# Keys and queries of the last two batches transposed by VectorE in 32x32 blocks instead of by TensorE

## The chip, the cores and the metric

The kernel runs on one core of a Trainium2 chip. The metric is the device time of one execution in microseconds; the median of three runs is given. The engines are named as in the profile: PE (TensorE, matrix products and their transpositions), PEld (its weight loads), DVE (VectorE), ACT (ScalarE), POOL (GpSimd) and SP (SyncE, which here only issues transfers). SBUF is the on-chip memory, PSUM the eight accumulator banks of PE.

## The reference

Attention with a sigmoid in place of a softmax feeds a gated product, and that feeds a soft mixture of experts. B = 4 batches, H = 12 heads, S = 448 tokens, D = 64.

```python
scores = q @ k.T / sqrt(64) - log(448)          # per batch and head, 448 x 448
x = sigmoid(scores) @ v                         # -> 1792 x 768 tokens
y = ((x @ w_a) * (x @ w_b)) @ w_out             # 768 -> 1536 -> 768
logits = y @ phi                                # 768 -> 32 slots
slot_in = softmax(logits, over tokens).T @ y    # 32 x 768, 4 slots for each of 8 experts
slot_out[e] = relu(slot_in[e] @ w1[e]) @ w2[e]
out = softmax(logits, over slots) @ slot_out
```

## The kernel before

Products are made in a split form: each operand is a high part (rounded) and a low part (the rest), and three products hi·hi, lo·hi, hi·lo are summed. So every K and Q is transposed, cast to `kh` or `qh`, and subtracted to `kl` or `ql`.

Attention is a generator, `att`, over 24 pairs g of heads (six a batch, pair g = 6b + p). For each pair:

- `load_qkv` loads K, Q and V three pairs ahead, from SP's queue, into rings of three buffers. K and Q lie in SBUF as 112 partitions by 4 chunks by 2 heads by 64, in runs of 256 bytes; K and V have four neighbouring tokens on one partition.
- `transposed` (L146) has PE turn the four 112x128 chunks into one PSUM bank of tag "ms" (L149), loads the next one, and sets the flag `run["trans"]`.
- `split_heads` makes the parts on DVE: `kh` at L142, `kl` at L143, and the same for Q. `emit_TK` does K, and for pairs above 12 Q as well; `emit_TQ` does Q of the earlier ones.
- `emit_S` (L183) makes the scores, chunk by chunk, two banks of tag "sc" for each (for chunk 2 of some pairs, tag "ab"), and ACT takes the sigmoid (L186).
- `emit_PV` (L196) makes 16 products with V into one "sc" bank, and `emit_x` copies the result (L219 on DVE, or ACT).

PSUM is shared by tags: four banks "sc", two "ms", two "ab", each handed out in turn, so that a new use of a bank waits for the last reader of the old one. In a pair from 13 on the order on PE is: K and Q of the next pair, chunk 0, PV of the last pair, chunks 1, 2, 3.

The pairs of batch 0 run first. Those of batch 1 are woven between the pieces of the gated product of batch 0, `ab(0)` (L520), until about 217 us. Batches 2 and 3 (pairs 12 to 23) follow nearly undisturbed until about 305 us; K and Q of pair 12 and 13 are still transposed inside `ab(0)`. Then come the products of batches 1 and 2 by a Strassen scheme (L692), `ab(3)`, and the experts, whose weights stream in from about 600 us on.

Until about 205 us DVE, ACT and POOL also bring the weights into another number format (L324, L328 on ACT, L335 to L337 on DVE, L342 on POOL), which is stored and loaded back and split (L436, L437).

The small work behind the gated product (group by group: adding to the logits at L475, transposing tokens at L489 with copies at L491, the first logits at L726, L750, L762, L771) is a list of generators, `fill`. After every step of attention or of `ab` one piece is taken from it by `fill_step`, unless that step has just transposed. The flag decides that:

```python
yield (fc * 12 + i * 6 + s * 2 + 2) / (KF * 12)
if not run.pop("trans", False):
    fill_step()
```

The dense loop over pairs 12 to 23 has the same two lines. Here a table of work does not set the order; the flag and the yields do.

Of the kernel before, what the change touches and what calls it, by code (L numbers as in the profile page):

```python
# [9 lines left out]
F32 = mybir.dt.float32  # L10
# [8 lines left out]
B, H, S, D = 4, 12, 448, 64  # L19
DM, FF, NS, NE, F = 768, 1536, 32, 8, 1024  # L20
C = 4
T = S // C
# [3 lines left out]
NP = H // 2  # L26
NE1, NE2 = 17, 4
ST0, PP, RAWS = 10, (3, 7), (2, 3, 10, 14)

LOW = 2.0 ** -15  # L30
HIGH = struct.unpack("f", struct.pack("I", 0x47EFFFFF))[0]
# [2 lines left out]
def body(ctx, tc, q, k, v, w_a, w_b, w_out, phi, w1, w2, out):  # L34
    nc = tc.nc
    pe, act, dve, pool, sp = nc.tensor, nc.scalar, nc.vector, nc.gpsimd, nc.sync
# [10 lines left out]
    atp = at_ctx.enter_context(tc.tile_pool(name="atp", bufs=1, side="right"))  # L47
# [14 lines left out]
    def ms(shape=(128, S)):  # L62
        tags = banks[run["banks"]]
        tag = tags[run["ms"] % len(tags)]
        run["ms"] += 1
        return ps_tile(tag, list(shape), 4 if tag == "sc" else 2)
# [49 lines left out]
    qkv_t = {}  # L116

    def load_qkv(g, names):
        if g >= B * NP:
            return  # L120
        b, p = divmod(g, NP)
        for src, nm, n in ((k, "k", 3), (q, "q", 3), (v, "v", 3)):
            if nm not in names:
                continue

            s = src[b, 2 * p:2 * p + 2].rearrange(
                "h (c p) d -> p h c d" if nm == "q" else "h (p c) d -> p h c d", c=C)
            if nm == "v":
                t = atp.tile([T, 2, C, D], F32, tag="vn", name="vn", bufs=n)
                sp.dma_start(out=t, in_=s)  # L130
            else:
                t = atp.tile([T, C, 2, D], F32, tag=nm + "n", name=nm + "n", bufs=n)
                for h in range(2):
                    sp.dma_start(out=t[:, :, h], in_=s[:, h])
            qkv_t[nm, g] = t
# [9 lines left out]

    def transposed(g, nm, t):  # L146
        a = qkv_t.pop((nm, g))
        for c in range(C):
            pe.transpose(t[:, c * T:(c + 1) * T], a[:, c].rearrange("p h d -> p (h d)"), ident[:T, :T])  # L149
        load_qkv(g + 3, nm)  # L150
        run["trans"] = True
        return t

    def emit_TK(g):
        if g >= B * NP:
            return
        both = g == 0 or g > 2 * NP
        tk = transposed(g, "k", ms())
        if both:
            tq = transposed(g, "q", ms())  # L160
        split_heads(g, "k", tk, dve.tensor_copy)
        if both:
            split_heads(g, "q", tq, dve.tensor_copy if g else act.copy)

    def emit_TQ(g):
        if g >= B * NP:
            return
        split_heads(g, "q", transposed(g, "q", ms()),
                    dve.tensor_copy)
# [43 lines left out]
    def emit_x(g):  # L213
        pv = pv_t.pop(g)
        qkv_t.pop(("v", g))
        b, kk = divmod(g, NP)
        if b:
            xt[g] = raw_x(b, kk)
            (act.copy if b == 1 else dve.tensor_copy)(xt[g], pv)  # L219
        else:  # L220
            xh = x0p.tile([128, S], F32R, tag=f"xh{kk}", name=f"xh{kk}")
            xl = x0p.tile([128, S], F32R, tag=f"xl{kk}", name=f"xl{kk}")
            act.activation(xh, pv, AF.Copy)
            dve.tensor_tensor(xl, pv, xh.bitcast(F32), op=ALU.subtract)
            xt[g] = (xh, xl)
        load_qkv(g + 3, "v")
# [693 lines left out]


    load_qkv(0, "qkv")
    consts()
    load_qkv(1, "qkv")
# [109 lines left out]
    for what in order0:  # L1034
        i = what[1]
        h, n, f0 = (0, 4, 4 * i) if i < 3 else (1, 6, 6 * (i - 3))
        for x in range(n):
            fc = f0 + x
            j = fc % 4
# [15 lines left out]
    for n in range(0, len(order1), 4):  # L1055
        _, g, x, _ = order1[n]
# [44 lines left out]
    for h in range(2):  # L1101
        for b in range(B):
            pl, nm = slots.pop(0)
# [4 lines left out]
    for h, (c0, w) in enumerate(COLS):  # L1108
# [4 lines left out]
        t = ms((128, w))  # L1113
        pe.matmul(t, selF.rearrange("p j s -> p (j s)"), s4[:, c0:c0 + w], start=True, stop=True)
        evac[h](s4r[:, c0:c0 + w], t)
        for c in range(C):
            op = []
            for b in range(B):
                tag = tags[k % 6]
# [35 lines left out]
```

## Time and profile before

| | |
|---|---|
| median of three runs | 702.97 us (702.44 to 703.36) |
| profiled execution | 703.76 us |
| its span in the trace | 702.0 us, mean granted clock 0.992 |
| PE busy | 657.9 us, 94% |
| PEld busy | 472.2 us, 67% |
| DVE busy | 368.4 us, 52% |
| POOL busy | 308.3 us, 44% |
| ACT busy | 297.6 us, 42% |
| chain that ended last | PE 66%, DMA 18%, DVE 6%, POOL 4%, ACT 2% |

The profile is of one execution, 0.8 us above the median; the time outside its span is 1.8 us. Busy shares are means over stages with different limits: a share of 52% may hide a stage in which an engine is always late.

### The profile page before, as it was taken

The page shows a single profiled execution, that of the slowest core. Times are in us where ns is not written, and L with a number is a line of the kernel's source. Part 1 is how long each engine was busy: PE and PEld are TensorE (multiplying, and loading weights), DVE is VectorE, ACT ScalarE, POOL GpSimd, SP SyncE. Part 2 cuts the span into 40 slices and gives each one's busy share as a digit, 9 for nine tenths or more (in the row PEclk, how much of TensorE's full clock was granted, in tenths as well). Part 3 has the DMA queues.
Part 4 walks back from the last instruction along what each step waited for, and adds up shares of the span by engine and source line. Part 5 has one row for each costly group of instructions (what it writes and reads, how often), then busy time and mean ns, then how long its engine had stood idle before and what let it go on. Part 6 is the DMA issues. An engine that isn't in the chain of part 4 may idle for free.

```text
span 702.0 us, 11034 instructions
## 1 busy us (share of the span) xinstructions
PE 657.9 (94%) x4187; PEld 472.2 (67%) x4187; DVE 368.4 (52%) x537; ACT 297.6 (42%) x536; POOL 308.3 (44%) x236
## 2 busy tenths in 40 slices
PE   6999999999999999999999999999998898997683
PEld 4557777777775555568988988998887786432132
DVE  4676899889754444449775675653322122300022
ACT  4888778779655465663333233202120011100021
POOL 0243767667644047339995575642333352000000
PEclk9999999999999999999999999999999999999997
DMA  9998999999834333201123323322999936999998
GB/s 197 254 294 215 278 312 302 279 278 304 245 120 129 71 98 77 71 0 46 46 85 103 99 73 98 116 68 80 256 391 413 379 114 240 374 416 415 409 350 276
DMA packets 104819, 146.90 MB, mean 209 GB/s; under 512 B 50880, under 2 KB 83904, under 8 KB 100800
## 3 DMA queue, kind: packets, MB, share of 16 engines
q1 hardware_dynamic: 101536, 139.81, 61.9%
q10 hardware_dynamic: 3232, 6.41, 2.7%
q8 instruction: 33, 0.54, 0.3%
q14 instruction: 18, 0.15, 0.1%
HBM read 122.69 MB, written 23.50 MB: 208 GB/s over the span
## 4 chain that ended last, share of the span: by engine, by line
PE 66%; DMA 18%; DVE 6%; POOL 4%; ACT 2%; issue 1%; SPq 0%; DVEq 0%; POOLq 0%; ACTq 0%
PE ab L520 15%; PE sc L692 14%; DMA e<-in_moe_w 9%; PE sc L196 9%; DMA wr<-ab 7%; PE ab L692 7%; PE sc L183 6%; PE ms L149 3%; PE ms L489 2%; DVE gk L337 2%; POOL wl L437 1%; PE ab L183 1%; DMA out<-w 1%; PE ms L471 1%; DVE gk L336 1%
## 5 line engine op out<-in xcount | busy, mean ns | idle before, releaser
L186 ACT ACTIVATE a<-sc,sums 112x448 f32<-112x448 f32 x158 | 89.0, 642 | 43.0 <-PE sc L183 42.7
L342 POOL TENSOR_TENSOR w<-gk,cy 128x768 int32<-128x768 int32 x36 | 66.2, 1840 | 91.5 <-DVE gk L337 59.6
L196 PE MATMUL sc<-a,vn 112*64 112x448 f32 x384 | 77.8, 546 | 1.0 <-ACT a L186 1.0
L437 POOL TENSOR_TENSOR wl<-wr,wh 128x768 fp32r<-128x768 f32 x22 | 40.5, 1842 | 68.3 <-DVE wh L436 43.2
L520 PE MATMUL ab<-t,wh 128*128 128x448 f32 x288 | 65.4, 372 | 5.3 <-DVE wh L436 5.3
L520 PEld LDWEIGHTS ab<-t,wh 128*128 128x128 f32 x288 | 52.8, 188 | 11.6 <-issue 5.3
L196 PEld LDWEIGHTS sc<-a,vn 112*64 112x64 f32 x384 | 25.7, 136 | 41.2 <-issue 34.8
L437 POOL TENSOR_TENSOR wl<-w,wh 128x768 fp32r<-128x768 f32 x24 | 44.3, 1848 | 2.5 <-ACT wh L436 2.5
L1086 PE MATMUL ab<-e,gk 128*32 128x384 f32 x240 | 33.3, 507 | 12.0 <-DMA e<-in_moe_w 12.0
L527 ACT COPY misc<-ab 128x448 f32<-128x448 f32 x24 | 12.8, 534 | 74.8 <-PE ab L520 38.6
L335 DVE TENSOR_SCALAR mf<-gk 128x768 f32<-128x768 f32 x36 | 34.1, 946 | 13.5 <-ACT gk L324 13.5
L183 PE MATMUL sc<-qh,kh 64*112 64x448 f32 x158 | 36.3, 429 | 1.1 <-ACT qh L142 0.6
L580 POOL TENSOR_TENSOR wx<-wr,wx 128x384 fp32r<-128x384 f32 x29 | 34.1, 1177 | 3.8 <-ACT wx L579 2.1
L436 DVE CAST wh<-wr 128x768 fp32r<-128x768 f32 x22 | 13.1, 594 | 42.3 <-DMA wr<-ab 41.1
L336 DVE TENSOR_SCALAR gk<-mf 128x768 uint32<-128x768 uint32 x36 | 34.3, 953 | 1.2
L520 PE MATMUL ab<-xh,wh 128*128 128x448 f32 x144 | 34.9, 378 | 0.0
L520 PE MATMUL ab<-xl,wh 128*128 128x448 f32 x144 | 34.5, 375 | 0.0
L520 PE MATMUL ab<-xh,wl 128*128 128x448 f32 x144 | 34.5, 375 | 0.0
L520 PE MATMUL ab<-t,wl 128*128 128x448 f32 x144 | 34.0, 372 | 0.0
L1086 PEld LDWEIGHTS ab<-e,gk 128*32 128x32 f32 x240 | 9.3, 112 | 35.0 <-DMA e<-in_moe_w 24.6
L580 POOL TENSOR_TENSOR wx<-T,wx 128x384 fp32r<-128x384 f32 x23 | 24.7, 1075 | 15.8 <-ACT wx L579 15.3
L520 PEld LDWEIGHTS ab<-xl,wh 128*128 128x128 f32 x144 | 26.0, 188 | 8.1 <-issue 6.3
(436 smaller groups left out, 1457.4 us busy)
## 6 DMA issues: line engine op xcount, KB each, us to landing
e<-in_moe_w SPq DMA_DIRECT2D x23, 1024.0 KB, 11.6
e<-in_moe_w SPq DMA_DIRECT2D x23, 768.0 KB, 15.1
wr<-ab SPq DMA_DIRECT2D x14, 768.0 KB, 4.8
ab<-w SPq DMA_DIRECT2D x24, 384.0 KB, 7.1
wr<-ab ACTq DMA_DIRECT2D x16, 384.0 KB, 7.5
kn<-in_k SPq DMA_DIRECT2D x48, 112.0 KB, 4.4
qn<-in_q SPq DMA_DIRECT2D x48, 112.0 KB, 4.1
vn<-in_v SPq DMA_DIRECT2D x24, 224.0 KB, 4.0
```

The lines of the kernel that those rows point to most:

```text
L149: pe.transpose(t[:, c * T:(c + 1) * T], a[:, c].rearrange("p h d -> p (h d)"), ident[:T, :T])
L183: pe.matmul(sc[h], kx[r, cs], qx[r], start=(i == 0), stop=(i == 2))
L186: act.activation(a, sc[h], AF.Sigmoid, bias=nlog[:T], scale=1.0 / math.sqrt(D))
L196: pe.matmul(pv_t[g][64 * h:64 * h + 64], qkv_t["v", g][:, h, c, :], a_t.pop((g, h, c)), start=(c == 0), stop=(c == C - 1))
L335: dve.tensor_scalar(mf, m, LOW, HIGH, op0=ALU.max, op1=ALU.min)
L336: dve.tensor_scalar(mi, mf.bitcast(U32), 3, 0x3FFFFFFF, op0=ALU.logical_shift_left, op1=ALU.bitwise_and)
L342: pool.tensor_tensor(thirds(w), m.bitcast(I32), thirds(cy_t.pop(x)), op=ALU.add)
L437: pool.tensor_tensor(wl, t, wh.bitcast(F32), op=ALU.subtract)
L520: pe.matmul(t, w[:, kk * 128:(kk + 1) * 128], xt[b * NP + kk][xi], start=(s == 0 and kk == 0), stop=(s == 2 and kk == KD - 1))
L580: pool.tensor_tensor(w[:, 1], t, w[:, 0].bitcast(F32), op=ALU.subtract)
L692: pe.matmul(t, w[:, wi, k * 128:(k + 1) * 128], xs[ORDER[m], k][xi], start=(s == 0 and k == 0), stop=(s == 2 and k == 2))
L1086: pe.matmul(sps[h][32 * j:32 * j + 32], hT[:, 2 * x + i, 2 * j + g], ring[order2[n + j]][0][:, i, c0:c0 + w], start=(g == 0 and x == 0 and ...
```

## The change

For pairs from GT0 = 12 on, K and Q are loaded by four transfers each: each fills 32 partitions with 14 runs of 32 numbers (128 bytes), so that one DVE instruction, `dve.transpose`, which turns every 32x32 block, gives the transposed 128x448 in the "ms" bank. V of these pairs is loaded in natural token order (runs of 256 bytes in place of 1 KB). `transposed` returns on that path without setting the flag.

```diff
+GT0 = 2 * NP
...
+            if g >= GT0:
+                if nm == "v":
+                    t = atp.tile([T, 2, C, D], F32, tag="vn", name="vn", bufs=n)
+                    sp.dma_start(out=t, in_=src[b, 2 * p:2 * p + 2].rearrange("h (c p) d -> p h c d", c=C))
+                else:
+                    t = atp.tile([128, 2 * C * D], F32, tag=nm + "n", name=nm + "n", bufs=n)
+                    t = t[:, :S].rearrange("p (n d) -> p n d", d=32)
+                    for j in range(4):
+                        sp.dma_start(out=t[32 * j:32 * j + 32],
+                                     in_=src[b, 2 * p + j // 2][:, j % 2 * 32:j % 2 * 32 + 32].rearrange(
+                                         "(n t) d -> t n d", t=32))
+                qkv_t[nm, g] = t
+                continue
...
-                t = atp.tile([T, C, 2, D], F32, tag=nm + "n", name=nm + "n", bufs=n)
+                t = atp.tile([128, 2 * C * D], F32, tag=nm + "n", name=nm + "n", bufs=n)
+                t = t[:T].rearrange("p (c h d) -> p c h d", c=C, h=2)
...
     def transposed(g, nm, t):
         a = qkv_t.pop((nm, g))
+        if g >= GT0:
+            dve.transpose(t, a.rearrange("p n d -> p (n d)"))
+            load_qkv(g + 3, nm)
+            return t
         for c in range(C):
             pe.transpose(t[:, c * T:(c + 1) * T], a[:, c].rearrange("p h d -> p (h d)"), ident[:T, :T])
         load_qkv(g + 3, nm)
```

Lines of the changed kernel stand some 15 to 19 further down: L142 is L157 there, L149 has no counterpart for these pairs (L164 on DVE), L183 is L202, L196 is L215, L337 is L356, L475 is L494, L489 is L508, L491 is L510, L520 is L539. A name's number is that of one allocation; allocations of one tag take its banks in turn, so `ms_2073` and `ms_2090` are one bank (two "ms" banks, `ms_2084` between them).

The first place is PE at K of pair 12, in `ab(0)`. The rows before, from the last L520 product ahead of K's transpositions to the group's transpositions behind PV:

```order
L520 MATMUL ab_2033<-xl5_752,wh2_1904 128x448
L149 MATMUL ms_2061<-ident_89,kn_1195 128x112 [waits DMAHW1_49,DMAHW0_49,DVE_49]
L149 MATMUL ms_2061<-ident_89,kn_1195 128x112 x3
L520 MATMUL ab_2033<-xh0_285,wl2_1905 128x448 [waits Pool_49]
...
L196 MATMUL sc_2087<-a_1919,vn_1228 64x448 [waits DMAHW4_49,Activation_49]
...
L489 MATMUL ms_2100<-ident_89,misc_95 112x128 [waits Activation_49]
L489 MATMUL ms_2100<-ident_89,misc_95 112x128 x3
L489 MATMUL ms_2106<-ident_89,misc_95 112x128 [waits DVE_49,PE_49]
L489 MATMUL ms_2106<-ident_89,misc_95 112x128 x3
```

And after:

```order
L539 MATMUL ab_2045<-xl5_752,wh2_1914 128x448
L508 MATMUL ms_2084<-ident_89,misc_95 112x128 [waits Activation_49]
L508 MATMUL ms_2084<-ident_89,misc_95 112x128 x3
L508 MATMUL ms_2090<-ident_89,misc_95 112x128 [waits DVE_49]
L508 MATMUL ms_2090<-ident_89,misc_95 112x128 x3
L539 MATMUL ab_2045<-xh0_285,wl2_1915 128x448 [waits Pool_49]
...
L215 MATMUL sc_2110<-a_1929,vn_1230 64x448 [waits DMAHW6_49]
```

The eight group transpositions move from behind PV to where K's four stood; their second four use the bank after K's and wait for DVE. The wait for POOL on the products behind them is the same.

The second place is DVE at the same point: the end of a weight's reformatting (L335 to L337), then the parts of K. Before:

```order
L335 TENSOR_SCALAR mf_2053<-gk_2_94 128x768 [waits Activation_49]
L336 TENSOR_SCALAR gk_2_94<-mf_2053 128x3x256 [waits DVE_49]
L337 SCALAR_TENSOR_TENSOR gk_2_94<-wr_all_96,gk_2_94 128x3x256 [waits DMAHW7_49,DVE_49]
L142 CAST kh_2069<-ms_2061 128x448 [waits PE_49]
L143 TENSOR_TENSOR kl_2070<-ms_2061,kh_2069 128x448 [waits DVE_49]
L530 TENSOR_TENSOR misc_95<-misc_95,ab_2033 128x448 [waits PE_49]
L491 COPY gk_01_93<-ms_2100 112x512 [waits PE_49]
```

And after:

```order
L354 TENSOR_SCALAR mf_2065<-gk_2_94 128x768 [waits Activation_49]
L355 TENSOR_SCALAR gk_2_94<-mf_2065 128x3x256 [waits DVE_49]
L356 SCALAR_TENSOR_TENSOR gk_2_94<-wr_all_96,gk_2_94 128x3x256 [waits DMAHW1_49,DVE_49]
L164 STREAM_TRANSPOSE ms_2073<-kn_1195 128x448 [waits DMAHW2_49]
L157 CAST kh_2080<-ms_2073 128x448 [waits DVE_49]
L158 TENSOR_TENSOR kl_2081<-ms_2073,kh_2080 128x448 [waits DVE_49]
L510 COPY gk_01_93<-ms_2084 112x512 [waits PE_49]
L549 TENSOR_TENSOR misc_95<-misc_95,ab_2045 128x448 [waits PE_49]
```

K's transposition is put between the reformatting and kh, and the copy of the group's tokens (L510) moves ahead of the product with the gate (L549).

The third place is PE in pair 14 (the transpositions are of pair 15), with the instructions of one shape drawn together. Before:

```order
L489 MATMUL ms<-ident,misc 112x128 x8
L149 MATMUL ms<-ident,kn 128x112 x4
L149 MATMUL ms<-ident,qn 128x112 x4
L183 MATMUL sc<-qh,kh 112x448 x2
L183 MATMUL sc<-qh,kl 112x448 x2
L183 MATMUL sc<-ql,kh 112x448 x2
L196 MATMUL sc<-a,vn 64x448 x8
L489 MATMUL ms<-ident,misc 112x128 x4
```

And after:

```order
L508 MATMUL ms<-ident,misc 112x128 x8
L202 MATMUL sc<-qh,kh 112x448 x2
L202 MATMUL sc<-qh,kl 112x448 x2
L202 MATMUL sc<-ql,kh 112x448 x2
L508 MATMUL ms<-ident,misc 112x128 x4
L215 MATMUL sc<-a,vn 64x448 x8
```

K's and Q's eight are gone, and the last four group transpositions move from behind PV to ahead of it.

## Rows read from the trace of the kernel before

**Rows 1.** Busy time by engine in one stretch: PE, PEld, DVE, ACT, POOL, clock, DMA, GB/s.

```profile
150.00:200.00 50.00, 48.97 (x302) 37.95 (x303) 43.53 (x51) 38.92 (x62) 33.31 (x19) 1.00 0.82 254
```

**Rows 2.** Timeline, 171 to 182 us: start, duration, engine, line, operation.

```profile
172.04 0.60 PE L149 MATMUL ms<-ident,kn 112*128 112x112 f32 x4 [0.22 <-DVE misc L475]
...
172.42 1.47 PE L520 MATMUL ab<-xh,wl 128*128 128x448 f32 x6
...
173.49 1.84 POOL L437 TENSOR_TENSOR wl<-w,wh 128x768 fp32r<-128x768 f32 x1
...
173.81 3.23 PE L196 MATMUL sc<-a,vn 112*64 112x448 f32 x16
173.87 2.28 DVE L337 SCALAR_TENSOR_TENSOR gk<-wr_all,gk 128x768 uint32<-128x768 uint32 x1
...
176.07 0.61 DVE L142 CAST kh<-ms 128x448 fp32r<-128x448 f32 x1
...
176.97 1.14 PE L489 MATMUL ms<-ident,misc 128*112 128x128 f32 x8
...
177.87 1.46 PE L520 MATMUL ab<-xh,wh 128*128 128x448 f32 x6
```

**Rows 3.** Timeline of PE, 192 to 202 us.

```profile
193.55 0.60 PE L149 MATMUL ms<-ident,qn 112*128 112x112 f32 x4 [0.24 <-ACT wT L368]
...
199.31 0.55 PE L149 MATMUL ms<-ident,kn 112*128 112x112 f32 x4
```

**Rows 4.** Timeline, 218 to 231 us.

```profile
218.24 0.39 DVE L603 CAST A12h<-t 128x448 fp32r<-128x448 f32 x1
...
224.56 0.52 ACT L750 COPY ls_d<-ab 128x448 f32<-128x448 f32 x1
...
225.54 0.46 PE L183 MATMUL ab<-qh,kh 64*112 64x448 f32 x2
...
226.95 1.08 PE L489 MATMUL ms<-ident,misc 128*112 128x128 f32 x8
...
227.63 1.29 DVE L491 COPY gk<-ms 112x512 f32<-112x512 f32 x2 [1.29 <-PE ms L489]
...
228.38 0.60 PE L149 MATMUL ms<-ident,kn 112*128 112x112 f32 x4 [0.35 <-DVE gk L491]
```

**Rows 5.** Timeline, 245 to 256 us.

```profile
253.77 0.60 PE L149 MATMUL ms<-ident,kn 112*128 112x112 f32 x4
...
254.69 0.46 PE L183 MATMUL sc<-qh,kh 64*112 64x448 f32 x2
...
254.81 1.70 ACT L186 ACTIVATE a<-sc,sums 112x448 f32<-112x448 f32 x3
...
255.51 0.20 PEld L196 LDWEIGHTS sc<-a,vn 112*64 112x64 f32 x4 [0.34 <-ACT a L186]
```

**Rows 6.** Costliest groups of the page: the sigmoids on ACT.

```profile
L186 ACT ACTIVATE a<-sc,sums 112x448 f32<-112x448 f32 x158 | 89.0, 642 | 43.0 <-PE sc L183 42.7
```

**Rows 7.** Timeline, 275 to 289 us.

```profile
281.38 0.46 PE L183 MATMUL sc<-qh,kh 64*112 64x448 f32 x1 [0.32 <-DVE t L219]
```

**Rows 8.** DMA queue in 247.3:254.2: packets, MB, share of 16 engines.

```profile
q1 hardware_dynamic: 2097, 0.69, 40.7%
```

**Rows 9.** The same view in 236:238.5.

```profile
q1 hardware_dynamic: 464, 0.06, 15.6%
```

**Rows 10.** Timeline of SP (DMA issues), 245 to 256 us.

```profile
254.41 1.23 SPq L134 DMA_DIRECT2D kn<-in_k  x2
```

**Rows 11.** Waits of SP, 440 to 620 us: total, times, longest.

```profile
SPq L428 <- PE sc L489: 12.4, 1, 12.4
```

**Rows 12.** Timeline of PE, 645 to 664 us.

```profile
651.45 2.77 PE L1086 MATMUL ab<-e,gk 128*32 128x384 f32 x28 [1.05 <-DMA e<-in_moe_w]
...
659.02 3.54 PE L1086 MATMUL ab<-e,gk 128*32 128x384 f32 x28 [0.42 <-DMA e<-in_moe_w]
```

**Rows 13.** Half a microsecond near the end, columns as in rows 1.

```profile
694.50:695.00 0.50, 0.00 (x0) 0.00 (x0) 0.00 (x0) 0.00 (x0) 0.00 (x0) 0.73 0.95 301
```

## The prediction

> **What bounds the kernel now.** I read the busy times of the stretches first, then the chain that ended last, then the timeline at each place the change touches. From 150 to 200 us PE is busy 48.97 of 50 us [rows 1], so what is put ahead of PE there goes through to the end unless something later swallows it. Nothing does: the later stages run on PE or on weight loads, and the long transfers in front of the last product leave SP only after SP has waited 12.4 us for PE's transpositions [rows 11]; a late PE makes them late by as much.
>
> From about 245 us the steady pairs are bound otherwise, though PE is nearly always busy there. In pair order PE does the K and Q transpositions of the next pair, chunk 0 of this pair, PV of the last pair, and chunks 1 to 3. PV's bank is the one that chunk 3, head 0 of the last pair had, four "sc" allocations back (seven a pair, four banks), so PV waits until ACT has done that sigmoid, the fifth after the PV before. The trace shows it: a sigmoid takes 0.642 us [rows 6], that one starts at 254.81 and so ends at 255.45, and PV's first weights go in at 255.51, with ACT named as what they waited for [rows 5]. The gap is 0.06 us.
>
> **Term A, the K of pair 12 (about 172 us): +5.1.** Before, PE issues K's four transpositions at 172.04, six matmuls of L520 at 172.42, PV at 173.81, eight transpositions of L489 at 176.97, and L520 again at 177.87 [rows 2]. After, `transposed` sets no flag, `fill_step` runs at once, and the eight L489 stand where K's four stood. They fill two "ms" banks. The second is the bank of K's transposition, free only when DVE has read kl out of it; PE's order shows the wait on DVE. DVE works in order: K's transposition stands behind the last bit operation of weight reformatting, L337, which starts at 173.87 and takes 2.28 [rows 2], to 176.15. Then come the transposition (0.6, below), kh (0.61, the cast at 176.07) and kl, which reads the same bank and is put at the same: 177.97. The first four L489 run before that, the second four (0.45, half of 176.97 to 177.87) from 177.97 to 178.42, L520 for 1.39 (172.42 to 173.81), PV for 3.16 (173.81 to 176.97): the next L520 starts at 182.97 in place of 177.87. That is 5.1 us late, with the gain from K's four already inside. Behind the waiting instruction stand all of PE's later products; no other order of PE's rows lets them pass.
>
> L337 is 2.28 here with POOL's L437 beside it from 173.49 to 175.33 [rows 2]. The Trainium skill (SBUF — State Buffer, Who interferes with whom) says that a DVE instruction with two SBUF inputs contends with GpSimd and one with at most one does not. L337 has two and agrees; by that rule the transposition itself, with one input, would keep its short price beside POOL, which no run here has shown yet.
>
> **The price of one DVE transposition: 0.6.** The trace has none. The nearest rows read or write the same 128x448 f32 through PSUM: the cast at 176.07 takes 0.61 [rows 2]. Below it lies the SBUF-only cast of the same shape, 0.39 [rows 4]; above, I allow twice the cast, about 1.25. I take 0.6, since kind and size of the data are the same. At 0.39 term A is 4.9; at 1.25 it is 5.8, and the terms on DVE below grow by about 3 in all.
>
> **Term B, Q of 12, K and Q of 13: −1.1.** One set of four costs PE 0.38 (172.04 to 172.42 [rows 2]); three sets at 193.55 and 199.31 [rows 3] go in the PE-bound stretch, 3 x 0.38 = 1.14. With the 0.24 that PE waited at 193.55 it would be 1.4.
>
> **Term C, pairs 14 to 16 (217 to 245 us): +0.6.** Here PE is not yet held by the sigmoids. A K and Q pair of sets frees 0.92 (253.77 to 254.69 [rows 5]), three times 2.8, and 0.35 of waiting at 228.38 [rows 4]. Against it stand two new waits. First, chunk 2 of pair 14 takes an "ab" bank which ACT frees with the copy at 224.56, done at 225.08 [rows 4]. That copy follows a DVE reduction which now stands behind two more transpositions (1.2, of which I let 0.85 through, the softmax's start having some slack): 225.93. PE would be there at 225.54 [rows 4] less 0.92: wait 1.3. Second, the four L489 that stood behind PV now stand ahead of it and must wait for pair 15's kl: DVE's two copies at 227.63 last 1.29 [rows 4] and move 0.4 with PE to 229.3; two transpositions, kh and kl end at 231.8; PE, after its eight L489 (226.95 plus 0.4) and chunk 0, is there at about 229.4: wait 2.4. Sum 1.3 + 2.4 − 2.8 − 0.35 = +0.55, taken as +0.6. Bounds: −3.1 if neither wait comes, +2 if the gain of pair 16 is lost too.
>
> **Term D, the steady pairs (245 to 302 us): 0.** Removing 0.92 of PE work brings chunk 0 forward, but PV still starts when the fifth sigmoid ends, and ACT has been working back to back from the first scores after the PV before [rows 5]. The freed time turns into idle PE, pair by pair. Cover gone (a sigmoid chain shorter than I read) it would be worth up to 0.92 a pair.
>
> **Term E, pairs beside POOL's Strassen operands (277 to 290 us): +0.2.** PE waits 0.32 at 281.38 for DVE's copy of x [rows 7], behind casts held by POOL. Two more DVE operations a pair (1.2) delay that copy, PE's own lateness and the idle time of DVE hide most. Bounds −2 and +2.4 (two pairs by 1.2).
>
> **Term F, the clock: +0.8.** The five idle microseconds of term A cost once more if TensorE's clock falls to its half level. At the end of the kernel it falls in the half microsecond after 694.5 (mean 0.73 [rows 13]), PE being idle; between loads of the last stage 28 matmuls took 3.54 at the low level and 2.77 at the high one [rows 12]. I take one such stretch, 0.77; bounds 0 and 1.6.
>
> **Transfers and SP: 0.** In a pair window the queue moved 2097 packets in 40.7% of 6.9 us on 16 engines, 21.4 ns a packet [rows 8]: 1792 of 256 bytes for K and Q, 224 of 1 KB for V. A store of 128-byte runs took 464 packets in 15.6% of 2.5 us, 13.4 ns each [rows 9]. After, K and Q are 3584 packets, and V, whose layout changes as well (token order now natural, runs of 256 bytes), 896. 4480 packets take 3.8 to 6.0 us of 6.9. SP needs 1.23 for two issues of 448 runs [rows 10]; eight and V's longer one are about 6 of 6.9. Both fit, and loads run three pairs ahead, but little is left over. While weights stream (150 to 205 us, DMA share 0.82 [rows 1]) a delayed weight load could cost more: 0 to +3.
>
> The Trainium skill (DMA: Bandwidth & Descriptors, Specifications) asks for at least 512 bytes for line rate and says that below it SDMA does read-modify-write: it speaks against this change, and gives rival 4. The two rows here show no dearer packet at 128 bytes than at 256; by the rule's own wording both sizes are already below it.
>
> **Sum.** 5.1 − 1.1 + 0.6 + 0 + 0.2 + 0.8 = +5.6. The profiled execution took 703.76 us (span 702.0), 0.8 above the median 702.97; added to the median: 708.6. My forecast is 708.5.
>
> **Rivals.**
> 1. Faster: the steady pairs give the time back, because the chain of sigmoids moves up with the scores. Nine pairs by 0.92 are −8.3, with the other terms +5.6: 700.3; without POOL's term and with C at −3.1, 696.4. For it: PE is the busiest engine there. Against: the 0.06 us in [rows 5]. It turns from loss to gain where more than six of nine pairs pay.
> 2. Stall A does not come, because DVE reaches K's transposition early, or is overtaken by later slack: 708.5 − 5.1 − 0.8 = 702.6. For it: L337 is 2.28 only through POOL. Even if it cost no more than the casts beside it, 0.61, the stall would keep 3.4, so this needs a mistake about the bank.
> 3. DVE's transposition costs 1.25: A +0.6, C and E +3: 712.
> 4. The short runs bind transfers: from 24.6 ns a packet (6.9 x 16 / 4480) they decide; at 30 ns a pair takes 8.4, +1.5 in each of eight pairs: 720.
>
> **Chances.** Forecast 0.60, rival 1 0.13, rival 2 0.09, rival 3 0.13, rival 4 0.05. The forecast's own range is 705 to 711. For 8 in 10 I leave out rival 4, nearly all of rival 1 and a little of rival 3: 702 to 713. A difference under 0.2% (1.4 us) can hardly be told from none: faster 0.14, same 0.09, slower 0.77.
>
> **What would show it.** In the new profile: PE idle for about 5 us near 172.5, ahead of the group transpositions, released by DVE kl; a transposition on DVE of about 0.6; PV in steady pairs still within 0.1 of a sigmoid's end, the pair still at 6.9 us, with PE idle of 0.9 in it; a lower clock in the half microseconds after 174; queue share under 90%. The prediction is wrong if steady pairs get shorter, if the eight group transpositions don't wait, or if pairs stretch to the pace of SP or the queue.

## The result and the profile after

The changed kernel takes 710.77 us (median of 4, 710.31 to 713.56) against 703.16 for the kernel before on the same chip: ratio 1.011, 95% interval 1.0081 to 1.014, so 7.6 us slower. The forecast was 5.5 slower (708.5, range 702 to 713). The profiled execution of the changed kernel took 713.56 us (span 711.8), the longest of the four; the profiled one of before took 703.76. The traces therefore show 9.8 us, and 2 of them more than the medians do.

The engines' line of the page of the changed kernel (busy us, share of the span, instructions):

```profile
PE 656.4 (92%) x4091; PEld 468.9 (66%) x4091; DVE 380.5 (53%) x561; ACT 296.8 (42%) x536; POOL 310.2 (44%) x236
```

PE has 1.5 us less to do than before and a longer span. Its longest waits between 150 and 330 us (engine and line that waited, what for, us in total, times, longest):

```profile
PE ms L508 <- DVE kl L158: 8.2, 2, 5.7
PE sc L215 <- ACT a L205: 3.5, 5, 0.7
PE sc L202 <- DVE t L238: 2.6, 2, 1.7
PE ab L202 <- ACT ls_d L769: 0.9, 1, 0.9
```

The first row did not exist before: two waits of the group transpositions for DVE's kl. The second is one in each of five steady pairs, up to 0.71 us long: there most of the freed time went (3.5 of 5 x 0.92 = 4.6 us).

To place the loss I took the start of each pair's PV from the timelines of both kernels and subtracted; the zero is PV of pair 9 (at 147 us), the last before the change acts. The columns of the table below are worked out in this way from one profiled execution each; in the runs whose code is that of before up to pair 13, the shift at pair 10 lies anywhere from −0.5 to +0.6 us, so that differences of about half a microsecond between rows say nothing.

| PV of pair | 10 | 11 | 12 | 13 | 14 | 19 | 20 | 22 |
|---|---|---|---|---|---|---|---|---|
| changed kernel | +8.1 | +6.1 | +5.2 | +8.2 | +8.1 | +8.1 | +7.6 | +10.4 |
| e1_flag | +0.4 | −0.1 | −1.0 | −0.3 | +2.1 | +2.1 | +1.6 | +2.6 |
| e2_order | +6.4 | +5.0 | +5.0 | +5.7 | +5.3 | +5.3 | +5.3 | +5.3 |
| e3_flag_pvab | −1.0 | −1.7 | −2.5 | −2.7 | −0.3 | −4.2 | −0.6 | +1.6 |
| e4_before_pvab | −0.2 | −0.2 | −0.2 | −0.2 | −0.2 | +0.8 | +1.2 | +3.2 |
| e5_late | −0.5 | −0.5 | −0.5 | −0.5 | −0.5 | −0.5 | −1.0 | +1.6 |
| e6_late_pvab | −0.5 | −0.5 | −0.5 | −0.4 | −0.4 | −3.6 | −3.0 | −2.0 |
| e7_17to20_pvab | +0.2 | +0.2 | +0.2 | +0.2 | +0.2 | −2.7 | −2.3 | −2.3 |
| e8_late_twice | +0.6 | +0.7 | +0.7 | +0.7 | +0.7 | +0.7 | +3.5 | +5.0 |
| e9_17to20 | −0.1 | 0.0 | 0.0 | 0.0 | 0.0 | 0.0 | −0.6 | −0.6 |
| e10_12_13_17to20_pvab | −0.3 | −0.8 | −0.8 | −0.8 | −0.8 | −3.8 | −3.4 | −3.4 |
| e11_17to19_pvab | −0.5 | −0.5 | −0.5 | −0.5 | −0.5 | −2.5 | −2.6 | −2.6 |

The loss of the changed kernel comes at three places: pair 10 (the stall at K of pair 12), pair 13 (K of pair 15), pairs 21 and 22. Between pairs 14 and 19 nothing is gained or lost. At the first place the timeline of the changed kernel answers to [rows 2]:

```profile
172.85 0.65 PE L508 MATMUL ms<-ident,misc 128*112 128x128 f32 x4 [0.59 <-ACT gk L510]
...
174.35 0.95 DVE L354 TENSOR_SCALAR mf<-gk 128x768 f32<-128x768 f32 x1 [1.25 <-ACT gk L343]
...
176.33 0.96 DVE L356 SCALAR_TENSOR_TENSOR gk<-wr_all,gk 128x768 uint32<-128x768 uint32 x1
177.20 0.65 DVE L164 STREAM_TRANSPOSE ms<-kn 128x448 f32<-128x448 f32 x1
...
177.89 0.62 DVE L157 CAST kh<-ms 128x448 fp32r<-128x448 f32 x1
...
178.55 0.62 DVE L158 TENSOR_TENSOR kl<-ms,kh 128x448 fp32r<-128x448 f32 x1
...
179.23 1.10 PE L508 MATMUL ms<-ident,misc 128*112 128x128 f32 x4 [5.73 <-DVE kl L158]
...
179.99 2.59 PE L539 MATMUL ab<-xh,wl 128*128 128x448 f32 x6
...
182.50 4.10 PE L215 MATMUL sc<-a,vn 112*64 112x448 f32 x16
...
186.53 1.48 PE L539 MATMUL ab<-xh,wh 128*128 128x448 f32 x6
```

The bit operations of the same weight began, in the kernel before, with this row:

```profile
171.91 0.94 DVE L335 TENSOR_SCALAR mf<-gk 128x768 f32<-128x768 f32 x1
```

PE issues the first four group transpositions at 172.85, then stands idle for 5.73 us until DVE has done kl. DVE's transposition costs 0.65. L337, here L356, takes only 0.96: POOL's split, which ran beside it before, ends here at 176.39, just as L356 starts. But DVE's first bit operation started at 174.35 (171.91 before), after 1.25 us of waiting for ACT. The stall then costs a second time. These are stretches of 2 us around it (busy time of PE, PEld, DVE, ACT, POOL; granted clock; DMA share; GB/s):

```profile
174.00:176.00 2.00, 0.00 (x0) 0.00 (x0) 1.61 (x2) 1.11 (x2) 2.00 (x2) 1.00 0.94 214
176.00:178.00 2.00, 0.00 (x0) 0.00 (x0) 1.93 (x4) 0.00 (x0) 0.88 (x2) 0.87 0.95 334
178.00:180.00 2.00, 0.77 (x5) 0.77 (x5) 1.74 (x3) 0.00 (x0) 1.32 (x1) 0.50 0.73 173
...
182.00:184.00 2.00, 2.00 (x6) 0.53 (x6) 1.39 (x2) 1.30 (x2) 1.60 (x1) 0.50 1.12 274
184.00:186.00 2.00, 2.00 (x12) 0.80 (x10) 1.93 (x3) 0.00 (x0) 0.00 (x0) 0.92 0.04 6
```

PE does nothing from 174 to 179; the clock is whole in the first of these rows, 0.87 in the second, at its half level (1.2 GHz) in the third and whole again, but for the start, in the last: six L539 take 2.59 us where they had taken 1.47 [rows 2]. From 179.23 to the next L539 at 186.53 PE needs 7.3 us for what took 0.45 + 1.39 + 3.16 = 5.0 before: +2.3 us by the clock.

The second place, pair 15, with the two waits that were forecast in term C:

```profile
232.66 0.46 PE L202 MATMUL ab<-qh,kh 64*112 64x448 f32 x1 [0.90 <-ACT ls_d L769]
...
237.68 0.62 DVE L158 TENSOR_TENSOR kl<-ms,kh 128x448 fp32r<-128x448 f32 x1
...
238.46 0.64 PE L508 MATMUL ms<-ident,misc 128*112 128x128 f32 x4 [2.46 <-DVE kl L158]
```

The "ab" bank comes 0.90 late by ACT's copy (1.3 forecast), and the four group transpositions wait 2.46 for kl (2.4 forecast). After that the clock falls again; PV of pair 13 takes 4.8 us (239.10 to 243.88 in the chain that ended last) in place of 3.2.

The steady pairs, which answer to [rows 5]:

```profile
257.28 3.23 PE L215 MATMUL sc<-a,vn 112*64 112x448 f32 x16 [0.71 <-ACT a L205]
...
264.18 2.10 PE L215 MATMUL sc<-a,vn 112*64 112x448 f32 x10 [0.71 <-ACT a L205]
```

PV starts at 257.28 and 264.18, 6.90 us apart as before, and each time PE has been idle for 0.71 until ACT was done with a sigmoid.

The third place, pairs 21 and 22, which answers to [rows 7]:

```profile
294.45 0.65 DVE L164 STREAM_TRANSPOSE ms<-kn 128x448 f32<-128x448 f32 x1
295.02 0.62 DVE L164 STREAM_TRANSPOSE ms<-qn 128x448 f32<-128x448 f32 x1
...
297.91 0.61 DVE L238 COPY t<-sc 128x448 f32<-128x448 f32 x1
...
298.58 0.46 PE L202 MATMUL sc<-qh,kh 64*112 64x448 f32 x1 [1.70 <-DVE t L238]
...
300.04 0.20 PEld L215 LDWEIGHTS sc<-a,vn 112*64 112x64 f32 x4 [0.36 <-ACT a L205]
```

DVE's two transpositions of the next pair (294.45, 295.02) stand ahead of its copy of x at 297.91. The bank of chunk 1 is freed by that copy, so PE waits 1.70, and the PV behind it, that of pair 21, takes 4.92 at the low clock.

### The profile page after: what moved, and what is told of

It is laid out like the page before. It is cut to its first block, busy times and chain, and to the rows that moved or that the text cites. A ratio compares the mean times of both kernels' runs of the same rounds, so it can differ in the third digit from the quotient of the medians.

```text
span 711.8 us, 10932 instructions
## 1 busy us (share of the span) xinstructions
PE 656.4 (92%) x4091; PEld 468.9 (66%) x4091; DVE 380.5 (53%) x561; ACT 296.8 (42%) x536; POOL 310.2 (44%) x236
## 4 chain that ended last, share of the span: by engine, by line
PE 69%; DMA 14%; DVE 5%; POOL 4%; ACT 4%; issue 2%; SPq 0%; DVEq 0%; ACTq 0%; POOLq 0%
PE ab L539 19%; PE sc L711 13%; PE sc L215 9%; DMA e<-in_moe_w 9%; PE ab L711 7%; PE sc L202 6%; PE ms L508 2%; DMA wr<-ab 2%; PE ms L168 1%; PE ab L202 1%; PE ms L490 1%; ACT a L205 1%; DMA out<-w 1%; DVE gk L356 1%; DMA ab<-w 1%
## 5 line engine op out<-in xcount | busy, mean ns | idle before, releaser
L215 PE MATMUL sc<-a,vn 112*64 112x448 f32 x384 | 82.0, 570 | 4.5 <-ACT a L205 4.5
L539 PE MATMUL ab<-t,wh 128*128 128x448 f32 x288 | 66.8, 378 | 3.2 <-DVE wh L455 3.2
L539 PEld LDWEIGHTS ab<-t,wh 128*128 128x128 f32 x288 | 54.2, 192 | 9.1 <-DVE wh L455 3.9
L215 PEld LDWEIGHTS sc<-a,vn 112*64 112x64 f32 x384 | 27.0, 143 | 48.3 <-issue 38.0
L202 PE MATMUL sc<-qh,kh 64*112 64x448 f32 x158 | 38.8, 426 | 3.3 <-DVE t L238 2.6
L539 PE MATMUL ab<-xh,wl 128*128 128x448 f32 x144 | 35.5, 383 | 0.0
L539 PE MATMUL ab<-xh,wh 128*128 128x448 f32 x144 | 34.9, 378 | 0.0
L539 PE MATMUL ab<-xl,wh 128*128 128x448 f32 x144 | 34.6, 376 | 0.0
L202 PE MATMUL sc<-qh,kl 64*112 64x448 f32 x158 | 34.1, 374 | 0.0
L539 PE MATMUL ab<-t,wl 128*128 128x448 f32 x144 | 34.0, 372 | 0.0
L202 PEld LDWEIGHTS sc<-qh,kh 64*112 64x112 f32 x158 | 17.3, 174 | 24.6 <-issue 13.6
L549 DVE TENSOR_TENSOR misc<-misc,ab 128x448 f32<-128x448 f32 x24 | 14.8, 617 | 34.6 <-PE ab L539 34.6
L202 PE MATMUL sc<-ql,kh 64*112 64x448 f32 x158 | 33.1, 367 | 0.0
```

Of the source, the lines that this page charges most:

```text
L202: pe.matmul(sc[h], kx[r, cs], qx[r], start=(i == 0), stop=(i == 2))
L215: pe.matmul(pv_t[g][64 * h:64 * h + 64], qkv_t["v", g][:, h, c, :], a_t.pop((g, h, c)), start=(c == 0), stop=(c == C - 1))
L539: pe.matmul(t, w[:, kk * 128:(kk + 1) * 128], xt[b * NP + kk][xi], start=(s == 0 and kk == 0), stop=(s == 2 and kk == KD - 1))
L549: dve.tensor_tensor(g, g, t, op=ALU.mult)
```

## The experiments

**The order on PE, from both sides.** In e1_flag the changed kernel keeps its flag; in e2_order the kernel before gives it up for pairs 12 to 23. Against the changed kernel:

```diff
             dve.transpose(t, a.rearrange("p n d -> p (n d)"))
             load_qkv(g + 3, nm)
+            run["trans"] = True
             return t
```

and, against the kernel before,

```diff
-        run["trans"] = True
+        run["trans"] = g < 2 * NP
```

> The changed kernel with the flag set on the path of VectorE's transpositions too, so that the small work keeps its old places. Theory (the loss is the order: group transpositions that now stand ahead of other work on PE and wait for DVE's kl): PE's 5.7 us and 2.5 us waits are gone, and 702 us is expected (700.5 to 704): 703.2 less 1.5 for the sets removed inside ab(0), less about 2 in pairs 14 to 16, plus some 2 us that the changed kernel lost in pairs 20 to 22. Rival (the 128-byte loads or the price of VectorE's transpositions are the loss): it stays at 708 or more.

> The kernel before, TensorE's transpositions and all loads kept, but the flag not set for pairs 12 to 23, so that the small work follows the transpositions at once. Theory (the order is the loss): K of pair 12 is read by DVE until 177.3 us, the second four group transpositions wait for it, 4.5 us and 0.8 for the clock: 708.5 us (707 to 710). Rival (the loss needs VectorE's transpositions or the short loads): within 1 us of 703.2.

e2_order took 708.62 us against 702.93 (ratio 1.0088, 1.0068 to 1.0109), as forecast. With TensorE's transpositions and the old loads the same wait stands at the same place, as its timeline shows:

```profile
172.78 0.60 PE L489 MATMUL ms<-ident,misc 128*112 128x128 f32 x4
...
174.24 2.15 DVE L337 SCALAR_TENSOR_TENSOR gk<-wr_all,gk 128x768 uint32<-128x768 uint32 x1
...
177.73 1.07 PE L489 MATMUL ms<-ident,misc 128*112 128x128 f32 x4 [4.35 <-DVE kl L143]
```

The four group transpositions that go into K's bank wait 4.35 us for kl. So the stall needs neither VectorE's transposition nor the short loads: the lost flag makes it. e1_flag took 705.47 us against 702.93 (ratio 1.0027, 1.0007 to 1.0046; its twelve runs spread from 701.12 to 708.52): 2.5 us above the kernel before where the changed kernel is 7.6 above, but not the 702 expected. In the table the stall at pair 10 is gone and pairs 11 and 12 gain 1.4, as term B has it; then 2.4 are lost at pair 14. There the order with the flag has a wait of its own:

```profile
238.05 0.66 DVE L164 STREAM_TRANSPOSE ms<-kn 128x448 f32<-128x448 f32 x1
...
239.78 0.62 DVE L158 TENSOR_TENSOR kl<-ms,kh 128x448 fp32r<-128x448 f32 x1
...
240.55 4.49 PE L791 MATMUL ms<-gk,ls_d 112*32 112x256 f32 x64 [1.95 <-DVE kl L158]
```

The first logits' products (L771 before, L791 here) use K's bank after VectorE's transposition and wait 1.95 us for kl, where they had waited 0.23 for it in the kernel before; PE then does them at the low clock, 4.49 us in place of 2.81. I had not foreseen it, since I had followed the new order only.

**The bank of PV.** e3_flag_pvab is e1_flag with PV's result in a bank of tag "ab" from pair 13 on, e4_before_pvab does the same to the kernel before.

```diff
-            pv_t[g] = ps_tile("sc", [128, S], 4)
+            pv_t[g] = ps_tile("ab", [128, S], 2) if g >= 13 else ps_tile("sc", [128, S], 4)
```

> e1_flag, and the result of PV from pair 13 on put into a bank of tag ab in place of sc, so that PV no longer waits for the fifth sigmoid. Theory (in the steady pairs the freed 0.92 us of TensorE is held back by the sigmoid that frees PV's bank): the pair falls from 6.9 to about 6.0 us, 7 to 8 us are gained over e1_flag, about 695 us (692 to 698). Rival (something else paces a pair at 6.9, ACT itself or the loads): as e1_flag, within 1.5 us.

> The kernel before with PV from pair 13 on in a bank of tag ab. Theory: in the kernel before TensorE has 6.9 us of work a pair and the sigmoid is only just in time, so the other bank gives nothing: 703 us (702 to 704.5), pairs still 6.9 us. Rival (the sigmoid alone sets the pair): the pair falls below 6.6 us and the time to under 700 us.

e3_flag_pvab took 703.94 us (ratio 1.0018, 1.0003 to 1.0034), not 695, and only 1.5 under e1_flag, about what the rival expected of the time. Its steady pairs did what the theory expected:

```profile
253.43 3.23 PE L216 MATMUL ab<-a,vn 112*64 112x448 f32 x16
...
259.55 2.85 PE L216 MATMUL ab<-a,vn 112*64 112x448 f32 x14
```

PV starts 6.12 us apart instead of 6.90, which shows that PV's bank had held the freed time back. But of the 3.9 us gained from pair 14 to pair 19, 3.6 are lost in the next one:

```profile
278.72 0.62 DVE L239 COPY t<-ab 128x448 f32<-128x448 f32 x1
...
279.40 0.71 PE L203 MATMUL ab<-qh,kh 64*112 64x448 f32 x1 [3.40 <-DVE t L239]
```

Now PE's chunk 2, which needs an "ab" bank too, waits 3.40 us for the copy of x out of it, and that copy stands in DVE's queue behind work that waits for POOL. e4_before_pvab took 706.37 us (ratio 1.0053, 1.0038 to 1.0069) where 703 was expected: its steady pairs are 7.1 us long (+1.0 in the table over the five from 14 to 19), so with TensorE's own transpositions the other bank gives nothing, as expected; the late pairs lose 2.4 more up to pair 22, with PE waiting up to 1.8 us for a sigmoid and 0.8 for the copy of x before it gets an "ab" bank, which was not expected.

**Steady pairs alone.** In e5_late the change begins at pair 17, where no small work is left and PE's order differs from before only by the sets removed; e8_late_twice does each of its transpositions twice; e9_17to20 leaves pairs 21 to 23 to TensorE.

```diff
-GT0 = 2 * NP
+GT0 = 17
```

In addition, for e8_late_twice:

```diff
-            dve.transpose(t, a.rearrange("p n d -> p (n d)"))
+            for _ in range(2):
+                dve.transpose(t, a.rearrange("p n d -> p (n d)"))
```

For e9_17to20, in addition to GT0 = 17, at both places:

```diff
-        if g >= GT0:
+        if GT0 <= g <= 20:
```

> The changed kernel with GT0 = 17: VectorE transposes only from pair 17 on, when the small work behind the gated product is done, so that TensorE's order is that of before with 14 sets of four less and nothing else moved. Theory (steady pairs are paced by the sigmoid that frees PV's bank): pairs stay at 6.9 us, about 0.5 us is lost among pairs 20 to 22, time within 0 to +1 us of before, 703.5. Rival 1 of the prediction (the freed 0.92 us a pair comes through): 7 pairs, 6 us faster, 697. Rival 4 (short transfers): pairs longer than 6.9 us, 706 or more.

> e5_late with every VectorE transposition done twice, which doubles its price and changes no result. Theory: in steady pairs DVE has more than 3 us to spare, the pair stays at 6.9 us; only pairs 20 to 22, where the copy of x stands behind DVE's transpositions, lose 1 to 2.5 us more: 705 us (704 to 706.5). Rival 3 of the prediction (the price of a transposition comes through everywhere): 1.2 us in each of seven pairs, 711 or more.

> VectorE transposes for pairs 17 to 20 only, PV in sc as in the kernel before. e5_late was 4.3 us slower by its median, and its trace places 2.1 us of that among pairs 20 to 22, where DVE's copy of x stands behind the transpositions of pairs 21 and 22. Theory (that is all of the loss, with what the late and slow-clocked work makes later on): with 21 to 23 left to TensorE the loss is gone, 702 us, within 0.8 of before. Rival (the short transfers or something else in the steady pairs costs too): half of it stays, 704 or more.

e5_late took 706.32 us (ratio 1.0062, 1.0049 to 1.0075). The pairs stay at 6.90 us, so rival 1 and rival 4 are out; but the loss is 4.3 us, not 0 to 1. Its timeline at pairs 21 and 22:

```profile
287.03 0.65 DVE L164 STREAM_TRANSPOSE ms<-kn 128x448 f32<-128x448 f32 x1
...
290.48 0.61 DVE L238 COPY t<-sc 128x448 f32<-128x448 f32 x1
...
291.15 0.46 PE L202 MATMUL sc<-qh,kh 64*112 64x448 f32 x1 [1.70 <-DVE t L238]
...
293.07 4.30 PE L215 MATMUL sc<-a,vn 112*64 112x448 f32 x16
```

Again the copy of x is late behind DVE's transpositions, PE waits 1.70, and the 16 products of PV, 3.23 before, take 4.30 at the low clock. The table has +2.1 in all between pairs 19 and 22 here and nothing in the steady pairs.

e8_late_twice took 708.79 us (ratio 1.0101, 1.0084 to 1.0118), 2.5 above e5_late; I had expected 705, and rival 3 had 711. In the steady pairs the doubled price doesn't show at all (the same +0.7 from pair 10 to 19); all of it comes at pairs 20 and 21:

```profile
277.91 1.35 DVE L165 STREAM_TRANSPOSE ms<-kn 128x448 f32<-128x448 f32 x2
...
279.17 1.31 DVE L165 STREAM_TRANSPOSE ms<-qn 128x448 f32<-128x448 f32 x2
...
283.29 0.61 DVE L239 COPY t<-sc 128x448 f32<-128x448 f32 x1
...
283.95 0.53 PE L203 MATMUL sc<-qh,kh 64*112 64x448 f32 x1 [3.27 <-DVE t L239]
```

Two transpositions take 1.35 and 1.31 (the groups hold two each), the copy of x comes at 283.29, and PE has waited 3.27 for it.

e9_17to20 took 702.68 us against 702.06 (ratio 1.0007, 0.9993 to 1.0021): no difference. So the whole loss of e5_late hangs on pairs 21 to 23, with VectorE's transpositions and the loads that belong to them, though its trace places only half of it directly; the 2.5 us that doubling the transpositions cost came in the late pairs as well. Four sets of eight are removed from PE here, 4 x 0.92 = 3.7 us of PE's work, and next to nothing comes out. Its longest waits of PE between 150 and 330 us:

```profile
PE sc L215 <- ACT a L205: 2.8, 4, 0.7
```

Four waits of 0.7 for the sigmoid: that is where 2.8 of the 3.7 went.

**A version that gains.** e6_late_pvab is e5_late with PV in "ab" for pairs 14 to 18 only; e7_17to20_pvab the same with e9_17to20's bounds; e10_12_13_17to20_pvab adds pairs 12 and 13 with the flag set; e11_17to19_pvab leaves pair 20 to TensorE.

```diff
-            pv_t[g] = ps_tile("sc", [128, S], 4)
+            pv_t[g] = ps_tile("ab", [128, S], 2) if 14 <= g <= 18 else ps_tile("sc", [128, S], 4)
```

and for e10_12_13_17to20_pvab, at both places where the bounds stand, and behind the transposition:

```diff
-        if GT0 <= g <= 20:
+        if g in (12, 13, 17, 18, 19, 20):
...
             load_qkv(g + 3, nm)
+            run["trans"] = True
             return t
```

> e5_late with PV of pairs 14 to 18 in a bank of tag ab, and in sc again from pair 19 on, where DVE's copy of x is late behind POOL. Theory: the four or five pairs whose transpositions are gone and whose PV has the other bank fall from 6.9 to 6.1 us: 3 to 4 us under e5_late, 700 us (698.5 to 701.5), under the kernel before. Rival (the gain is paid back by later waits, as in e3_flag_pvab): 703 or more.

> e6_late_pvab with VectorE's transpositions for pairs 17 to 20 only; TensorE does those of 21 to 23, where DVE's extra work had delayed the copy of x by about 1 us. Theory: about 0.5 us under e6_late_pvab, 699.5 us. Rival (those pairs lose nothing by DVE's transpositions): 1 us or more above it, since TensorE has the work again.

> e7_17to20_pvab with pairs 12 and 13 transposed by VectorE too, with the flag set, so that the small work keeps its place. Theory (inside ab(0), where TensorE is the bound, each removed set is worth 0.38 us and nothing waits once the order is kept): 1.0 to 1.5 us under e7_17to20_pvab, 699 us. Rival (the extra DVE work there delays the weights and the gain is lost): within 0.5 us of e7_17to20_pvab or above it.

> e7_17to20_pvab with pair 20 left to TensorE as well. Theory (DVE's extra work beside POOL's operands is what lengthened the pairs that end at 274 and 282 us by 0.2 and 0.4 us, and TensorE waits there anyway): 0 to 0.6 us under e7_17to20_pvab, 699.8. Rival (the set removed from pair 20 is worth its 0.92 us): 0.9 above it.

e6_late_pvab took 704.25 us (ratio 1.0026, 1.001 to 1.0042): 2.1 under e5_late, but not 700, and above the rival's 703; the steady pairs gain 3.2 in its trace and the late ones give 1.6 back, and the profiled execution (701.7) was the fastest of twelve, so the trace shows less than was lost. e7_17to20_pvab took 700.08 us against 702.05 (ratio 0.9969, 0.9957 to 0.998): the first version under the kernel before, and by 4.2 us under e6_late_pvab where 0.5 was expected; TensorE's transpositions in the last three pairs are worth that. e10_12_13_17to20_pvab took 698.94 us against 702.06 (ratio 0.9955, 0.994 to 0.997), as expected, 3.1 us faster than the kernel before. It is 1.1 under e7_17to20_pvab, but the two ran on different chips and their intervals overlap, so that pairs 12 and 13 bring something isn't shown by the times. Its longest waits of PE:

```profile
PE ms L169 <- ACT wT L388: 0.9, 1, 0.9
PE ms L509 <- DVE kl L158: 0.9, 1, 0.9
PE sc L203 <- DVE t L239: 0.7, 1, 0.7
```

The table has the 0.5 us of pair 11 from the sets removed in the gated product, and 2.9 from pairs 14 to 19. e11_17to19_pvab took 700.89 us (ratio 0.9991, 0.9975 to 1.0007): it can't be told from the kernel before, nor clearly from e7_17to20_pvab, so whether pair 20 is better on VectorE stays open.

## Why the prediction was right, and where its sizes were off

The direction and the mechanism were right; the sum was 5.6 and the medians show 7.6. By the trace, whose own difference is 9.8 (which of the terms is smaller in the shorter executions isn't shown):

- **Term A**, +5.1: at the next L539, 186.53 against 177.87, the kernel is 8.1 late (less the 0.57 by which it was late at pair 9), 2.3 of it by the clock, so 5.8. The idle time forecast at the second four, up to 177.97, ended at 179.23 in a run that was 0.6 late already. Two errors met in it: L337 was not stretched this time, and DVE started its bit operations later, after a wait for ACT. e1_flag and e2_order show the cause, the place of the group transpositions.
- **Term B**, −1.1: from that L539 to PV of pair 11 the kernel wins 2.0. About 0.5 of this shows in e2_order without any set removed (5.5 late at L520 behind PV of pair 10, at 184.12, and 5.0 at PV of pair 11; the 6.4 in the table holds 0.9 for the eight group transpositions that stand ahead of PV there). What was late had some slack to catch up; e1_flag wins 1.4 between pairs 10 and 12, e10_12_13_17to20_pvab 0.5.
- **Term C**, +0.6: measured +2.0 (pair 11 to 14). Both waits were there in about the forecast size (0.90 and 2.46 against 1.3 and 2.4); the rest is mostly the low clock after the second, 1.6 in PV of pair 13.
- **Term D**, 0: measured 0.0 in five pairs, and shown from three sides: pairs unchanged at 6.90 with transpositions removed, unchanged with their price doubled, and 6.12 when PV got another bank.
- **Term E**, +0.2: measured +2.3. This is the step that failed most for its size. I wrote that PE's lateness and DVE's idle time hide most of two more operations; they hide next to nothing, because DVE starts its whole row of work for the pair only when POOL lets a cast go, and the copy of x is the last of that row. From the first of these casts to the copy DVE needed 4.00 us (293.91 to 297.91) where it had needed 2.93 (284.69 to 287.62). PE waited 0.89 and 1.70 for the copies of two pairs. The upper bound, +2.4, had the size, but 1.7 of what was measured is the low clock in PV of pair 21, which that bound had not counted.
- **Term F**, +0.8: mis-sized. It was counted once, at a row from the last stage. The trace has it at three places: 2.3 after the stall, 1.6 in PV of pair 13 (4.8 in place of 3.2), 1.7 in PV of pair 21 (4.92 in place of 3.23); the last two are inside the measured C and E. The row of 3.54 that 0.77 was taken from was at the half level only for its first 1.6 us, until about 660.6.
- **That nothing swallows a late PE** was nearly so: from +10.4 at pair 22 the trace falls to 9.2 at the end (9.8 less the 0.6 by which it was late at pair 9). In the last product PE's waits for DVE's split of weights fell from 5.3 to 3.2 us.
- **The sum** came nearer than its terms, and that is in part luck: A with the clock after it, C and E were 12.4 in the trace against 6.7 forecast; B and the end of the kernel gave back 3.2 against 1.1, and the other three executions were 2.5 to 3.3 us shorter than the profiled one.
- **Transfers**, 0: held. The queue (packets, MB, share of 16 engines) in 7 us of the steady pairs of the changed kernel, from 252 on, and in four whole pairs, from 257.28 to 284.88:

```profile
q1 hardware_dynamic: 6265, 0.89, 73.5%
...
q1 hardware_dynamic: 18471, 2.76, 56.7%
```

The first holds 1.4 pairs' packets; over whole pairs the share is 56.7%, against 40.7% before [rows 8]. That is 0.735 x 7 x 16 / 6265 = 13.1 ns a packet in the first and 13.6 in the second, against 21.4 before [rows 8] and 13.4 in the store of 128-byte runs [rows 9]. The rule of the Trainium skill (DMA: Bandwidth & Descriptors, Specifications) is that short transfers fall off line rate. The trace agrees in direction: while it was busy the queue moved 2.76 MB in 0.567 x 27.6 us, 176 GB/s, where it had moved 0.69 MB in 0.407 x 6.9 us, 246 GB/s. But no pair got longer by it, so it cost nothing here.

- **The price of a transposition**, 0.6: 0.65 and 0.62. Rival 3 is out; in the steady pairs even twice the price doesn't show, and it counts where PE waits for what stands behind it, kl at the first two places and the copy of x at the third. What the prediction left open is shown too: beside POOL the price stays. At 225.46 and 226.02 two transpositions ran wholly while POOL was at work, and took 0.65 and 0.62. The sentence of the Trainium skill (SBUF — State Buffer, Who interferes with whom) on instructions with at most one SBUF input excepts DVE's two-port modes, which the prediction left out.

Open stays where half of e5_late's 4.3 us lies: the trace of one execution places 2.1 at pairs 20 to 22, and e9_17to20 shows that all of it goes with those transpositions.

## What to carry to other kernels

Work that is taken off an engine that is always busy gains only if that engine also sets the pace: here PE was busy all of the time, yet ACT freed the PSUM bank for PV only 0.06 us before PE took it, and the gain came only when PV got another bank. When a step moves to another engine, look at what its absence moves: a flag, a yield or a queue's order that hung on it can put other work ahead of a wait, and that was the larger part of this loss. On an engine that works in order, a new operation costs what it delays of the work behind it, which here was nothing in the steady pairs and several microseconds in two late ones; put such work only where nothing that others wait for is last in the row.

## What the runs showed of the hardware that was not expected

A wait of PE can cost more than its length: after 5.73 us of idling the granted clock was at half until about 184 and added 2.3. After a shorter wait it is not the same each time. Behind a wait of 1.70 PV took 4.92 in the changed kernel and 4.30 in e5_late, in place of 3.23; in e1_flag, behind a wait of 1.69 at the same place, and in e6_late_pvab, behind 1.94 and 1.68, it took 3.23:

```profile
293.14 0.46 PE L203 MATMUL sc<-qh,kh 64*112 64x448 f32 x1 [1.69 <-DVE t L239]
...
294.60 3.23 PE L216 MATMUL sc<-a,vn 112*64 112x448 f32 x16
```

These are two microseconds of each, e5_late first, behind the wait (columns as above; the clock is third from the end):

```profile
292.00:294.00 2.00, 2.00 (x11) 0.85 (x9) 1.93 (x5) 2.00 (x4) 0.00 (x0) 0.50 0.44 175
...
294.00:296.00 2.00, 2.00 (x15) 0.82 (x13) 1.93 (x5) 2.00 (x4) 0.00 (x0) 1.00 0.46 183
```

So the length of the wait alone does not tell whether the clock falls. Whether executions of one kernel differ for this reason, as those of e1_flag do, isn't shown. The 0.71 in every steady pair left the clock whole. Packets that are mostly of 128 bytes took 13.1 to 13.6 ns, less by the packet than the mostly 256-byte ones that they replaced, so that more than twice as many raised the queue's share only from 40.7% to 56.7%. VectorE's transposition of 128x448 f32 into PSUM takes 0.62 to 0.65 us, as long as a cast of the same size out of it.
